# An attention and expert kernel whose order is planned: no filler matmuls before the first turning of keys, and 366 priorities set anew

## The chip, the core and the metric

The kernel runs on one core of one Trainium2 chip. A core has five engines that run side by side and wait for one another by semaphores: TensorE (PE in the profile, its weight loads apart as PEld), VectorE (DVE), ScalarE (ACT), GpSimd (POOL) and SyncE (SP), which issues most of the DMA transfers. Each engine takes its instructions strictly in the order in which the program holds them. The metric is the time of the launch in device microseconds, as the median of the runs.

## What is computed

Two stages, of which the second works on the result of the first. For each of four batches, 49 agents attend to 11456 keys and values, and then the queries attend to the agents; every token of the result goes to one of eight experts, the one with the largest logit, and through that expert's two layers.

```python
B, N, C = (4, 11456, 128)                      # 49 agents
def _attn_ref(q, k, v, agents):
    def sm(a, b):
        s = scale * (a @ b.transpose(0, 2, 1))
        e = np.exp(s - s.max(-1, keepdims=True))
        return e / (e.sum(-1, keepdims=True) + 1e-09)
    return sm(q, agents) @ (sm(agents, k) @ v)
...
logits = x @ w_gate                            # x: the result, 45824 x 128; 8 experts, hidden 1024
expert_idx = np.argmax(logits, axis=1)
for e in range(E):
    h = np.maximum(x[expert_idx == e] @ w1[e], 0.0)
    out[expert_idx == e] = gate_w[expert_idx == e, None] * (h @ w2[e])
```

## The kernel before

**Tiling.** A batch's 11456 tokens are cut into 12 chunks (11 of 1024 tokens as 128 partitions by 8, and a rest of 192). `key_chunk` adds the work of one chunk of keys: a load of k and one of v (512 KB each), two *turnings* of four 128x128 blocks each by TensorE (`turn`, line 593, in the first batch into a PSUM bank called px), their copies to SBUF by VectorE and ScalarE (`turned`, line 601), the scores of the agents against the keys (`kscores`, line 614), the running maximum (line 619), the exponentials (line 631), a turning back (`eback`, line 637) and the product with the values (`values`, line 652), which is added up in `acc`. Only three buffers (`vt`) hold values, so the load of chunk c+3 waits for `values` of chunk c. When all 12 are done, `agentvalues` (named av 0 to av 10) finishes the agents' values and multiplies them with the gate; `choose` finds the batch's commonest expert, whose weights are loaded. The steps named w (lines 905 to 1100) rewrite that expert's layers so that most tokens can pass through a small version of it. Queries are scored against the agents (lines 743 to 776), exponentiated (781), split in two halves (789, 794), turned by DMA into the tiles `M`, and routed (`logits`, line 838; `route`, lines 851 to 864).

**The expert stage.** `layer1` (L1, lines 1648 and 1649), `upper` and `lower` (lines 1655 and 1660), `linear` (L0) and `layer2` (L2, both line 1664), `store` (line 1709) and `put` run for 23 groups of 512 tokens per batch; `check` (ck, cx, lines 1677 and 1682) finds tokens for which the small version is not exact. Those, and the tokens of other experts, are gathered in 20 blocks of 128 rows (`prepare_blocks`, named g, lines 1437 to 1504) that go through the full layers (b1, bu, b2, lines 1525 to 1543). The stages of the four batches overlap: while batch b is in its expert stage, the attention of b+1 runs between.

**What sets the order.** Nothing is ordered by hand. Every step is added to a `Plan` with a rank, an engine, a planned cost, the steps it waits for and the buffers that it takes and frees. `Plan.order` walks through planned time: whenever an engine is free it takes the ready step of the lowest rank. The list that comes out is the program's order. Ranks come from a few numbers per part (`KS1, KT1`, `QA`, `RG`, `CK0`, `CK3`, `LTL`, `STAGES`) plus a table, `SHIFT`, that moves single steps. Planned costs and times decide the order alone; the chip takes its own time.

**Fillers.** Where TensorE would be idle in planned time for more than `FILL_GAP`, a spare matmul without use, `warm` (line 461 until the first linear, later line 465), is put into its row, so that the engine stays busy. They start in planned time zero, when the constant tile `place` that they read is the only thing they need.

Of the kernel before, what the change touches and what calls it, by code (L numbers as in the profile page):

```python
# [44 lines left out]
KS, KT, KS1, KT1 = -102.41, 5.86, -136.97, 9.15  # L45
KS0, KT0 = -300, 4
QA, QC, QC3, QA1, QA3 = -30.13, 6.23, 4.1, -23.65, -25.3
QD = (0, 0.5, 1, 1.5, 2, 5, 5.3, 5.8, 6.2, 6.6, 6.9)
LL, RG = 2.23, 1.22
# [5 lines left out]
CK0, CK1, CK2, CK3 = -0.61, 7.51, 2.21, 3.19  # L55

LT, LTS, LTL = 73.41, 2, 37.18
# [6 lines left out]
STAGES = ((2, 11, -69.39, -69.39 + 6, 4.97, -2.93, 5.65), (3, 6, 20.99, 20.99 + 2, 10, 63.79, 4.01), (4, 3, 30.77, 30.77 + 2, 0, 85.1, 3.87))  # L64
# [5 lines left out]
FILL, FILL_GAP = 0.25, 0.15  # L70
STICK = 1.91
# [14 lines left out]
    (1, 'w', 'c0'): 2.73, (1, 'qwhole', 3): 2.73, (1, 'ehigh', 2): 2.73, (2, 'kmax', 1): 2.73, ('L0', 1, 14): 1.69, (1, 'put', 13): 1.69,  # L86
    ('cx', 1, 8, 1): 1.69, (1, 'enorm', 11): 1.69, (2, 'eback', 11): 1.69, ('L2', 74): 1.69, (1, 'eturn', 10): 1.69, (2, 'ecopy', 11): 1.69,
# [4 lines left out]
    (0, 'estore', 0): -0.44, ('ranks', 2, 0, 3): -3.38, (1, 'kcorr', 9): -3.86, ('cx', 0, 10, 0): 13.27, (1, 'qexp', 0): 13.27,  # L92
    (1, 'ehigh', 0): 13.27, (2, 'route', 8, 3): 0.71, (2, 'qexp', 10): 0.71, ('L1', 121): 0.71, (2, 'ehigh', 10): 0.71, (2, 'factors', 8): 0.71,
# [6 lines left out]
    (0, 'w', 'lm'): -0.16, (0, 'route', 0, 3): -0.16, (0, 'factors', 0): -0.16, (1, 'kmax', 0): -0.16, (0, 'eback', 9): 0.84, ('cx', 1, 5, 1): 6.52,  # L100
# [3 lines left out]
    (3, 'estore', 3): -12.27, ('L1', 157): -1.69, ('L2', 27): -1.76, (0, 'enorm', 11): -1.76, (0, 'estore', 11): -1.76, (1, 'vsum', 10): -1.76,  # L104
# [13 lines left out]
}  # L118


class Plan:
# [24 lines left out]
    def order(self):  # L146
# [9 lines left out]
        turn = {p: [] for p in self.strict}  # L156
# [35 lines left out]
        while left:  # L192
# [4 lines left out]
            for g in engines:  # L197
# [15 lines left out]
                e = best  # L213
# [1713 lines left out]
```

## Time and profile before

| | us |
|---|---|
| median of 3 runs | 730.42 (728.89 to 731.21) |
| the profiled execution, whole | 726.68 |
| its span, first to last instruction | 725.0 |
| TensorE busy | 673.6 (93%) |
| VectorE busy | 551.1 (76%) |
| ScalarE busy | 499.8 (69%) |
| GpSimd busy | 272.2 (38%) |

The profiled execution was 3.74 us shorter than the median of the timed runs. In the rows further below a time is in microseconds from the start of the span; a row of the timeline has start, duration, engine, line, operation, tiles written and read, and in brackets how long the engine was idle before it and what ended that. Rows of stretches give each engine's busy time, then the clock that the throttle granted TensorE as a share of 2.4 GHz, the share of the 16 DMA engines, and GB/s.

### The profile page before, as it was taken

What the parts mean: (1) busy time and instruction counts of PE and PEld (TensorE: products, weight loads), DVE (VectorE), ACT (ScalarE), POOL (GpSimd) and SP (SyncE); (2) the same over time, 40 slices, a digit from 0 to 9 for tenths busy, and PEclk for the clock granted to TensorE, in tenths of its full rate; (3) what the DMA queues carried; (4) which work ended last, traced back from release to release, by engine and by line L of the source; (5) the groups of instructions that cost most, each with busy time, mean ns of one, the idle gap of its engine ahead of it and who ended that gap; (6) DMA issues with size and microseconds to landing.
All of it is one profiled execution on the core that took longest, in us unless ns stands there. A gap on an engine that the chain in (4) does not pass through costs nothing. (4 is left out here: it accounts for less than half of the span.)

```text
span 725.0 us, 20869 instructions
## 1 busy us (share of the span) xinstructions
PE 673.6 (93%) x7844; PEld 528.2 (73%) x7844; DVE 551.1 (76%) x1545; ACT 499.8 (69%) x1145; POOL 272.2 (38%) x454
## 2 busy tenths in 40 slices
PE   7999899999999999999999999989699999999993
PEld 3675477777776677777767776676588788989992
DVE  4558767778789777688897888788998699987630
ACT  2555579997775889887766989868554997633330
POOL 1002313222168403111586053355888245241331
PEclk9999999999999999999999999999989999999997
DMA  8946999997492899997846999978967999876850
GB/s 296 332 142 185 271 236 239 289 233 230 140 308 84 239 306 253 285 186 208 272 127 172 285 255 274 242 186 230 247 180 185 237 244 239 209 236 211 257 177 16
DMA packets 219928, 162.11 MB, mean 224 GB/s; under 512 B 110363, under 2 KB 193661, under 8 KB 219824
## 3 DMA queue, kind: packets, MB, share of 16 engines
q1 hardware_dynamic: 216400, 156.41, 81.1%
q0 software_dynamic: 2240, 3.29, 2.5%
q8 instruction: 63, 1.03, 0.6%
q10 hardware_dynamic: 1184, 1.05, 0.5%
q14 instruction: 41, 0.34, 0.2%
HBM read 98.51 MB, written 36.82 MB: 187 GB/s over the span
## 5 line engine op out<-in xcount | busy, mean ns | idle before, releaser
L1664 PE MATMUL py<-W,hh 128*128 128x128 f16 x2160 | 146.2, 220 | 0.1
L1660 DVE SCALAR_TENSOR_TENSOR hh<-ph,hh 128x512 f16<-128x512 f32 (+1 forms) x184 | 121.5, 670 | 29.8 <-ACT hh L1655 29.5
L1664 PEld LDWEIGHTS <-hh 128*128 128x128 f16 x2160 | 129.6, 99 | 12.1 <-issue 7.8
L1655 ACT ACTIVATE hh<-ph 128x512 f16<-128x512 f32 (+1 forms) x184 | 106.6, 591 | 34.0 <-PE ph L1649 33.9
L1682 ACT ACTIVATE jk<-ps_small 128x512 f16<-128x512 f32 x180 | 108.7, 604 | 15.6 <-PE ps_small L1677 13.9
L799 POOL TENSOR_TENSOR sq<-E 128x392 f32<-128x392 f32 (+1 forms) x48 | 41.9, 874 | 205.2 <-ACT E L781 205.2
L1709 DVE TENSOR_TENSOR yo<-py,cs 128x512 f32<-128x512 f32 (+1 forms) x92 | 61.8, 671 | 15.3 <-PE py L1664 14.9
L601 ACT COPY xT<-ps_small 128x512 f32<-128x512 f32 (+1 forms) x99 | 55.5, 591 | 19.1 <-PE ps_small L593 19.0
L1648 PE MATMUL ph<-M,Wah 128*128 128x512 f16 (+1 forms) x162 | 60.7, 375 | 2.7 <-DVE hh L1660 2.4
L1649 PE MATMUL ph<-M,Wal 128*128 128x512 f16 (+1 forms) x162 | 60.7, 374 | 0.0
L593 PE MATMUL ps_small<-ident,ld 128*128 128x128 f32 x390 | 56.9, 276 | 3.9 <-DMA ld<-in_k_dram 2.4
L1677 PE MATMUL ps_small<-Wck,M 128*128 128x256 f16 x318 | 54.4, 273 | 2.0 <-ACT jk L1682 1.5
L1664 PEld LDWEIGHTS <-M 128*128 128x128 f16 x636 | 40.1, 98 | 21.4 <-issue 16.9
L1664 PE MATMUL py<-Wl,M 128*128 128x128 f16 x636 | 49.3, 220 | 5.5 <-DVE yo L1709 5.3
L593 PEld LDWEIGHTS ps_small<-ident,ld 128*128 128x128 f32 x390 | 43.7, 142 | 12.3 <-issue 3.8
L794 POOL TENSOR_TENSOR mm<-E,mm 128x392 f16<-128x392 f32 (+1 forms) x48 | 43.2, 902 | 19.5 <-ACT mm L789 11.3
L652 PE MATMUL ps_small<-vt,SS 128*49 128x129 f32 (+1 forms) x720 | 49.5, 278 | 0.9 <-ACT SS L643 0.5
L614 PE MATMUL ps_small<-xT,agf 128*64 128x512 f32 (+3 forms) x192 | 48.2, 579 | 1.3 <-ACT xT L601 1.1
L652 PEld LDWEIGHTS ps_small<-vt,SS 128*49 128x49 f32 (+1 forms) x720 | 39.1, 130 | 11.8 <-issue 4.2
L1677 PEld LDWEIGHTS <-M 128*128 128x128 f16 x318 | 28.7, 98 | 23.2 <-issue 10.1
L631 ACT ACTIVATE ET<-ps_small,nm 113x512 f32<-113x512 f32 (+1 forms) x48 | 31.6, 661 | 18.2 <-DVE nm L621 16.2
L1531 ACT ACTIVATE hs<-ph 128x512 f32<-128x512 f32 x40 | 23.3, 597 | 28.7 <-PE ph L1525 28.7
(335 smaller groups left out, 1551.8 us busy)
## 6 DMA issues: line engine op xcount, KB each, us to landing
ld<-in_k_dram SPq DMA_DIRECT2D x44, 512.0 KB
vt<-in_v_dram SPq DMA_DIRECT2D x44, 512.0 KB
ld<-in_q_dram SPq DMA_DIRECT2D x44, 512.0 KB
out_dram<-yo SPq DMA_DIRECT2D x88, 256.0 KB
w1e<-in_moe_w_dram SPq DMA_DIRECT2D x23, 512.0 KB
w2e<-in_moe_w_dram SPq DMA_DIRECT2D x23, 512.0 KB
exps<-E SPq DMA_DIRECT2D x44, 196.0 KB
ranks<-C SPq DMA_DIRECT2D x4, 724.0 KB
```

The source lines that it names most:

```text
L593: nc.tensor.transpose(pt[:, i * p:(i + 1) * p], x[:p, h + i, :], ident[:p, :p])
L601: (nc.scalar.copy if eng == "A" else nc.vector.tensor_copy)(TT[src, c][:, h:h + n, :p], pv)
L614: nc.tensor.matmul(ps[64 * j:64 * j + w, :n * p], AG["f"][:, :w], x[:, j * n:(j + 1) * n, :p], start=True, stop=True)
L652: nc.tensor.matmul(ps[r:r + w, :D + 1], s[:p, i, r:r + w], x[:p, j * n + i, :], start=i == 0, stop=i == n - 1)
L1648: nc.tensor.matmul(ph[:, :nn], st['ah'][:, f, :], m, start=True, stop=False)
L1649: nc.tensor.matmul(ph[:, :nn], st['al'][:, f, :], m, start=False, stop=True)
L1655: nc.scalar.activation(hh[:, 0, :nn], ph[:, :nn], AF.Relu)
L1660: nc.vector.scalar_tensor_tensor(hh[:, 1, :nn], ph[:, :nn], 0.0, hh[:, 0, :nn], op0=ALU.max, op1=ALU.subtract)
L1664: mm_ = lambda o, l, r, **k: nc.tensor.matmul(o, l, r, skip_group_check=True, **k)
L1677: nc.tensor.matmul(ps[:p, i * (FD - FN):(i + 1) * (FD - FN)], st['M'][c][:, 2 * j + i, :p], st['ck'].rearrange("a f p -> a (f p)"), start= ...
L1682: nc.scalar.activation(jk[:p, :2 * (FD - FN)], hs.pop(("c", c, j))[:p, :2 * (FD - FN)], AF.Relu, scale=-1.0, accum_out=st["fl"][:p, 4 * c ...
L1709: nc.vector.tensor_tensor(yo[:p, :n, :], py[:p, :n * D].rearrange("p (i d) -> p i d", d=D), cs.unsqueeze(2).broadcast_to([p, n, D]), op=AL ...
```

## The change

Two lines of `Plan.order` and its numbers. (a) No filler goes in until `FILL_FROM`, the second turning of the first chunk of keys, has been placed (`self.begun`). (b) TensorE counts as busy in planned time until 2.4. (c) Nine numbers of parts change (`KS1`, `KT1`, `QA`, `RG`, `CK0`, `CK3`, `LTL` and the ranks in `STAGES`), and the table `SHIFT` is replaced by one with 366 entries, of which a line is shown.

```diff
-KS, KT, KS1, KT1 = -102.41, 5.86, -136.97, 9.15
+KS, KT, KS1, KT1 = -102.41, 5.86, -130.54, 8.69
-QA, QC, QC3, QA1, QA3 = -30.13, 6.23, 4.1, -23.65, -25.3
+QA, QC, QC3, QA1, QA3 = -28.84, 6.23, 4.1, -23.65, -25.3
...
+PE_FROM, FILL_FROM = 2.4, (0, "turn", "k", 0, 4)
...
+    ('L2', 35): -2.03, ('L1', 161): -0.53, ('L0', 3, 10): -0.53, ('L2', 158): -0.53, ('L2', 159): -0.53, ('L1', 162): -0.53, ('b1', 9, 0): -1.75,
...
+        self.begun = False
...
         busy = {g: 0.0 for g in engines}
+        busy["PE"] = PE_FROM
...
+                self.begun = self.begun or e["name"] == FILL_FROM
...
-            if busy["PE"] <= t + 1e-9 and min(nxt) - t > FILL_GAP:
+            if self.begun and busy["PE"] <= t + 1e-9 and min(nxt) - t > FILL_GAP:
```

The work is the same but for the spare matmuls: 104 before, 87 now (66 and 53 of line 461 and its successor, line 492; 38 and 34 of the later kind). All lines behind the table stand 31 lines further down. What moves is shown at three places, before and then now.

TensorE, the start of the program: `sa` holds the agents' squares, `ag` the agents, `ld` a chunk of keys. Ten spares stand ahead of the first of these rows and three more behind the last.

```order
L461 LDWEIGHTS place
L461 MATMUL warm<-place 128x512
L514 MATMUL ps_small<-sa,ones 128x1
L515 MATMUL ps_small<-ident,ag 128x49
L461 LDWEIGHTS place
L461 MATMUL warm<-place 128x512
```

```order
L545 MATMUL ps_small<-sa,ones 128x1
L546 MATMUL ps_small<-ident,ag 128x49
L624 MATMUL px<-ident,ld 128x128 x8
L492 LDWEIGHTS place
L492 MATMUL warm<-place 128x512
```

Fourteen spares ahead of the first eight turnings are gone; the four behind them stay, and so do the next four.

ScalarE, batch 3, where its agents' values are finished while batch 2 is in its expert stage: `gj` squares the gate product, `E` and `mm` are the query exponentials and their upper half.

```order
L1655 ACTIVATE hh<-ph 128x512
L601 COPY xT<-ps_small 128x512
L789 CAST mm_160<-E 128x8x49
L781 ACTIVATE E<-E,ln_70,div 128x392
L789 CAST mm_161<-E 128x8x49
L702 ACTIVATE gj,gss<-ps_small 128x8
```

```order
L1713 ACTIVATE jk,fl<-ps_small 96x512
L1686 ACTIVATE hh<-ph 128x512
L733 ACTIVATE gj,gss<-ps_small 128x8
L735 COPY ava<-ps_small 49x128
L1686 ACTIVATE hh<-ph 128x512 x2
L812 ACTIVATE E<-E,ln_70,div 128x392
```

`gj` stood behind an exponential and its halves and now stands ahead of them.

VectorE, the same place a little later: `fm`, `fgt` belong to a block being prepared, `mq` and `E` to a chunk of queries, and L412 (now L443) is the first of the instructions that make `Gs`, the split gate that `logits` multiplies.

```order
L1477 TENSOR_TENSOR fm<-fm,fg 128x270
L1478 TENSOR_REDUCE fgt<-fm 128x3
L551 TENSOR_SCALAR hb<-ss 128x1
L771 TENSOR_REDUCE mq<-ps_small 128x4
L772 TENSOR_TENSOR E<-ps_small,mq 128x196
L771 TENSOR_REDUCE mq<-ps_small 128x4
L772 TENSOR_TENSOR E<-ps_small,mq 128x196
L412 TENSOR_SCALAR hb<-ps_small 128x1
```

```order
L1508 TENSOR_TENSOR fm<-fm,fg 128x270
L1509 TENSOR_REDUCE fgt<-fm 128x3
L443 TENSOR_SCALAR hb<-ps_small 128x1
L446 TENSOR_SCALAR mul<-hb 128x1
L449 TENSOR_SCALAR div<-hb 128x1
```

Five instructions on queries no longer stand between the block and the gate.

## Rows read from the trace of the kernel before

**Rows 1.** Busy time by stretch: columns as told above, PE to POOL
```profile
19.00:50.00 31.00, 31.00 (x300) 22.16 (x300) 17.82 (x43) 18.17 (x43) 0.00 (x0) 1.00 0.84 265
57.40:91.90 34.50, 30.32 (x261) 18.16 (x261) 26.96 (x94) 20.89 (x39) 11.42 (x22) 1.00 0.88 247
91.90:706.00 614.10, 584.44 (x7093) 469.01 (x7092) 492.55 (x1355) 450.83 (x1045) 255.27 (x408) 0.99 0.88 227
```

**Rows 2.** Waits of TensorE between 91.9 and 706: in total, times, longest
```profile
PE py L1664 <- DVE yo L1709: 5.5, 10, 1.9
PE ps_small L838 <- DVE Gs L716: 3.5, 1, 3.5
```

**Rows 3.** Timeline of TensorE, first 13 us
```profile
4.89 4.18 PE L461 MATMUL warm<-place 128*128 128x512 f16 x10 [4.89 <-DVE place L365]
...
9.31 1.04 PE L461 MATMUL warm<-place 128*128 128x512 f16 x4
...
10.18 1.04 PE L593 MATMUL px<-ident,ld 128*128 128x128 f32 x8
...
11.06 1.03 PE L461 MATMUL warm<-place 128*128 128x512 f16 x4
...
12.01 1.07 PE L614 MATMUL ps_small<-xT,agf 128*64 128x512 f32 x4
```

**Rows 4.** Timeline of VectorE and ScalarE there: the agents and the copies of turned keys
```profile
2.89 0.22 DVE L501 TENSOR_SCALAR ag<-ag 49x128 f32<-49x128 f32 x1 [0.57 <-DMA ag<-in_agents_dram]
...
3.37 0.19 ACT L510 ACTIVATION_READ_ACCUMULATOR jk<-ag 49x1 f32 x1
...
11.26 0.59 ACT L601 COPY xT<-px 128x512 f32<-128x512 f32 x1 [6.73 <-PE px L593]
```

**Rows 5.** Busy time by stretches at the start; here the last two columns count, the DMA's
```profile
0.00:4.00 4.00, 0.00 (x0) 0.00 (x0) 2.35 (x17) 1.69 (x3) 2.14 (x19) 1.00 0.36 76
4.00:8.00 4.00, 3.11 (x8) 1.26 (x9) 0.93 (x8) 0.32 (x1) 0.00 (x0) 1.00 0.99 323
8.00:12.00 4.00, 4.00 (x23) 2.27 (x20) 1.67 (x6) 0.59 (x1) 0.39 (x2) 1.00 1.08 340
12.00:28.00 16.00, 15.91 (x137) 10.98 (x137) 8.40 (x17) 8.64 (x19) 0.00 (x0) 1.00 1.07 374
```

**Rows 6.** Timeline of TensorE: values of chunk 3, of chunk 10, the first expert matmul
```profile
32.62 1.10 PE L652 MATMUL ps_small<-vt,SS 128*64 128x129 f32 x16
...
51.00 1.31 PE L652 MATMUL ps_small<-vt,SS 128*64 128x129 f32 x20 [0.35 <-DMA vt<-in_v_dram]
...
91.88 0.39 PE L1648 MATMUL ph<-M,Wah 128*128 128x512 f16 x1
```

**Rows 7.** Busy time of TensorE by the turnings of line 593 alone
```profile
19.00:50.00 31.00, 9.98 (x74) 7.85 (x73) 1.00 0.84 265
```

**Rows 8.** Timeline of TensorE where batch 3's agents' values are finished
```profile
517.65 0.38 PE L707 MATMUL ps_small<-gss,ones 128*128 128x1 f32 x2 [2.05 <-ACT gj L702]
...
524.77 0.36 PE L838 MATMUL ps_small<-Gs,M 128*128 128x18 f16 x8 [3.55 <-DVE Gs L716]
```

**Rows 9.** Timeline of VectorE there, from the agents' sum to the gate
```profile
511.31 0.22 DVE L693 TENSOR_REDUCE avs<-av 128x1 f32<-128x64 f32 x1
511.44 1.28 DVE L571 SCALAR_TENSOR_TENSOR hl<-ld,mul,hl 128x1024 f16<-128x1024 f32 x1
...
522.31 0.14 DVE L551 TENSOR_SCALAR hb<-ss 128x1 int32<-128x1 int32 x1
...
523.70 0.15 DVE L412 TENSOR_SCALAR hb<-ps_small 128x1 int32<-128x1 int32 x1
...
524.59 0.68 DVE L1660 SCALAR_TENSOR_TENSOR hh<-ph,hh 128x512 f16<-128x512 f32 x1
```

**Rows 10.** Stretches around two low grants of the clock
```profile
472.90:476.30 3.40, 3.37 (x36) 3.33 (x36) 2.41 (x7) 2.05 (x6) 2.81 (x6) 0.50 0.57 161
524.10:530.90 6.80, 5.93 (x35) 5.88 (x36) 6.40 (x20) 1.93 (x5) 6.38 (x10) 0.50 0.82 246
```

More of the change, by code (lines that the diff above doesn't have):

```diff
@@ L43 @@
 WHOLE = ((0, 1, 2), (0, 1, 2, 3, 4), (0, 1, 2, 3, 4), (0, 2, 4, 6, 8))
-KS, KT, KS1, KT1 = -102.41, 5.86, -136.97, 9.15
+KS, KT, KS1, KT1 = -102.41, 5.86, -130.54, 8.69
 KS0, KT0 = -300, 4
-QA, QC, QC3, QA1, QA3 = -30.13, 6.23, 4.1, -23.65, -25.3
+QA, QC, QC3, QA1, QA3 = -28.84, 6.23, 4.1, -23.65, -25.3
 QD = (0, 0.5, 1, 1.5, 2, 5, 5.3, 5.8, 6.2, 6.6, 6.9)
-LL, RG = 2.23, 1.22
+LL, RG = 2.23, 1.26
 TE = -14.49
@@ L54 @@
 LAG = 3
-CK0, CK1, CK2, CK3 = -0.61, 7.51, 2.21, 3.19
-LT, LTS, LTL = 73.41, 2, 37.18
+CK0, CK1, CK2, CK3 = -0.59, 7.51, 2.21, 3.38
+LT, LTS, LTL = 73.41, 2, 34.5
 RC = 9
@@ L63 @@
 PACE = (2, 4)
-STAGES = ((2, 11, -69.39, -69.39 + 6, 4.97, -2.93, 5.65), (3, 6, 20.99, 20.99 + 2, 10, 63.79, 4.01), (4, 3, 30.77, 30.77 + 2, 0, 85.1, 3.87))
+STAGES = ((2, 11, -70.36, -70.36 + 6, 4.76, -2.66, 5.75), (3, 6, 23.98, 23.98 + 2, 10, 63.79, 2.77), (4, 3, 27.31, 27.31 + 2, 0, 85.48, 4.91))
 HIGH = (0, 1, 2, 3)
 FILL, FILL_GAP = 0.25, 0.15
+PE_FROM, FILL_FROM = 2.4, (0, "turn", "k", 0, 4)
 STICK = 1.91
@@ L80 @@
 SHIFT = {
[5 rows of a table removed]
-    (1, 'w', 'c0'): 2.73, (1, 'qwhole', 3): 2.73, (1, 'ehigh', 2): 2.73, (2, 'kmax', 1): 2.73, ('L0', 1, 14): 1.69, (1, 'put', 13): 1.69,
-    ('cx', 1, 8, 1): 1.69, (1, 'enorm', 11): 1.69, (2, 'eback', 11): 1.69, ('L2', 74): 1.69, (1, 'eturn', 10): 1.69, (2, 'ecopy', 11): 1.69,
[4 rows of a table removed]
-    (0, 'estore', 0): -0.44, ('ranks', 2, 0, 3): -3.38, (1, 'kcorr', 9): -3.86, ('cx', 0, 10, 0): 13.27, (1, 'qexp', 0): 13.27,
-    (1, 'ehigh', 0): 13.27, (2, 'route', 8, 3): 0.71, (2, 'qexp', 10): 0.71, ('L1', 121): 0.71, (2, 'ehigh', 10): 0.71, (2, 'factors', 8): 0.71,
[6 rows of a table removed]
@@ L100 @@
-    (0, 'w', 'lm'): -0.16, (0, 'route', 0, 3): -0.16, (0, 'factors', 0): -0.16, (1, 'kmax', 0): -0.16, (0, 'eback', 9): 0.84, ('cx', 1, 5, 1): 6.52,
[3 rows of a table removed]
-    (3, 'estore', 3): -12.27, ('L1', 157): -1.69, ('L2', 27): -1.76, (0, 'enorm', 11): -1.76, (0, 'estore', 11): -1.76, (1, 'vsum', 10): -1.76,
[13 rows of a table removed]
[3 rows of a table added]
+    ('ranks', 0, 0, 2): 2.73, (2, 'turned', 'k', 1): 2.73, (1, 'qmax', 2): 2.73, (0, 'put', 20): 2.73, ('up', 45): 2.73, (2, 'eback', 0): 2.73,
+    ('lo', 45): 2.73, (1, 'qexp', 2): 2.73, (1, 'w', 'm'): 2.73, ('L0', 0, 21): 2.73, (1, 'w', 'sq'): 2.73, ('ranks', 0, 0, 3): 2.73,
@@ new lines @@
+    ('L2', 42): 2.73, (1, 'estore', 2): 2.73, (1, 'w', 'cp'): 2.73, (1, 'w', 'u'): 2.73, ('L2', 43): 2.73, (1, 'w', 's2'): 2.73,
+    (2, 'kscores', 1): 2.73, ('ranks', 0, 0, 4): 2.73, (2, 'ecopy', 0): 2.73, (1, 'w', 'c0'): 2.73, (1, 'qwhole', 3): 2.73, (1, 'ehigh', 2): 2.73,
[3 rows of a table added]
+    ('ranks', 3, 0, 12): -0.77, ('lo', 164): -0.77, ('ranks', 3, 0, 13): 1.97, (3, 'store', 11): 1.97, (3, 'qscores', 11): 9.66, ('L2', 151): 9.66,
[4 rows of a table added]
+    (0, 'kscores', 4): -0.78, (0, 'kmax', 3): -0.78, (0, 'values', 2): -0.78, (0, 'kmax', 4): -0.78, (0, 'kexp', 3): -0.56, (0, 'kcorr', 3): -1.34,
[3 rows of a table added]
@@ new lines @@
+    ('ck', 1, 6, 3): 3.79, (2, 'kcorr', 8): 3.79, (2, 'eback', 8): 3.79, (1, 'squares', 10): 3.79, (1, 'store', 9): 3.79, ('L1', 72): 3.79,
+    (1, 'put', 9): 3.79, ('L0', 1, 10): 3.79, (2, 'ecopy', 8): 3.79, (1, 'hb', 10): 3.79, (1, 'scaling', 10): 3.79, ('L2', 66): -0.21,
+    ('cx', 1, 6, 1): 3.79, (1, 'upper', 10): 3.79, (2, 'values', 8): 3.79, ('up', 70): 3.79, (2, 'turn', 'k', 9, 0): 3.79, (1, 'lower', 10): 3.79,
[5 rows of a table added]
+    ('ranks', 2, 0, 6): -0.39, (3, 'turn', 'q', 6, 0): -0.39, (3, 'ehigh', 3): -0.39, (3, 'estore', 4): -0.39, (3, 'turn', 'q', 6, 4): -0.39,
[3 rows of a table added]
@@ new lines @@
+    (2, 'estore', 5): 0.1, (3, 'load', 'k', 7): 0.1, (2, 'turn', 'q', 7): 0.1, (2, 'eturn', 0): 5.96, (1, 'put', 18): 5.96, (2, 'load', 'q', 3): 5.96,
[21 rows of a table added]
+    (0, 'turn', 'k', 2, 4): 2.55, (0, 'eback', 1): 2.55, (0, 'turn', 'k', 3, 0): 2.55, (0, 'kscores', 2): 2.55, (0, 'values', 1): 2.55,
+    (0, 'turn', 'k', 3, 4): 2.55, (0, 'turn', 'k', 4, 0): 2.55, (0, 'turn', 'k', 4, 4): 2.55, (0, 'eback', 2): 2.55, (3, 'turned', 'k', 4): 1.76,
+    ('L0', 2, 2): 1.76, ('up', 99): 1.76, ('L2', 96): 1.76, ('cx', 2, 2, 0): 1.76, ('lo', 99): 9.71, (3, 'values', 3): 1.76, (2, 'squares', 6): 1.76,
@@ new lines @@
+    ('L2', 24): 0.56, ('L1', 59): -0.19, (1, 'qscores', 6): -0.19, (2, 'values', 5): -0.19, (2, 'kscores', 6): -0.19, ('L2', 57): -0.19,
+    ('ck', 1, 3, 2): -0.19, ('L1', 60): -0.19, (3, 'qmax', 4): -1.68, (2, 'turn', 'k', 2, 0): -0.75, (0, 'qexp', 10): -0.37, (2, 'eback', 7): -0.48,
+    (2, 'kscores', 5): -1.68, (1, 'turn', 'q', 7): -1.68, ('ck', 1, 3, 0): -1.68, (0, 'turned0', 'k', 10): -0.24, ('b1', 19, 1): -13.15,
+    ('b2', 19): -13.15, ('up', 162): 0.27, (2, 'logits', 8): -0.7, ('L1', 120): -0.7, (3, 'kscores', 11): -0.7, ('L0', 2, 12): -0.7,
@@ L118 @@
+    (3, 'eback', 10): -0.7, ('L2', 116): -0.7, (0, 'vsum', 2): 0.22, (0, 'load', 'v', 5): 0.22, (0, 'kexp', 4): 0.22, (0, 'eback', 3): 0.22,
+    (0, 'turned0', 'k', 5): 0.22, (1, 'turned', 'k', 11): -8.96, ('bu', 13, 0): -1.37, ('cx', 2, 2, 1): 0.11, (3, 'kexp', 4): 0.11,
+    (3, 'kcorr', 4): 0.11, ('up', 101): 0.11, (3, 'ecopy', 4): 0.11, (2, 'squares', 7): 0.11, (0, 'put', 2): -5.81, ('up', 4): -3.35,
+    ('up', 5): -3.35, (0, 'qexp', 4): -3.35,
 }
```

72 rows, old and new, of the table SHIFT are left out of this document.

## The prediction

> **What bounds the kernel now.** I read the busy times of each engine first, then by stretch, then what TensorE waits for, and then the timeline wherever a wait or an idle stretch is moved by the change. TensorE is busy 93% of the span, and the stretches show how evenly: in the first batch's keys it has no idle time at all (31.00 of 31.00), and in the expert stages 584.44 of 614.10, so that 29.66 us of waits are all there is to win between 91.9 and 706 [rows 1]. Those waits are scattered; ten of them, for the buffer that `store` frees, make 5.5, the longest 1.9, and a single one, for the split gate `Gs`, makes 3.5 [rows 2]. VectorE, at 76%, decides TensorE's time only where something stands in its row ahead of what TensorE needs. So the time is TensorE's row of work plus its waits plus what it loses at the low clock, and a start that comes x earlier is worth x, if nothing behind eats it.
>
> The start is the other loss. TensorE's first useful matmuls stand behind ten spares: these run from 4.89 to 9.07, and the first eight turnings of keys run only from 10.18, with four more spares ahead of them; their four behind, then the first scores at 12.01 [rows 3]. The spares show the clock: the ten take 0.42 us each, the later four 0.26 each with the end of the last, so the clock stands at the lower level (1.2 GHz) through nearly all of the ten and at the upper (2.4 GHz) from about 9 on. (The clock column reads 1.00 throughout there; I go by the spacing.)
>
> **(a) and (b): no spares ahead of the first turnings.** When could these start? They need the first chunk of keys. The agents come first in TensorE's row, and their inputs are there early: VectorE had the agents at 2.89, ScalarE their squares by 3.56 [rows 4]. The chunk's landing isn't in the rows by itself, but the bytes are: 0.30 MB moved by 4.0, 1.29 more by 8.0 [rows 5]. The first key chunk is the first of the 512 KB loads (0.52 MB); with the small constants ahead of it, it is moved at about 4 + 0.25/0.323 = 4.8 if served in order, and later if the loads share the engines. What lies between the last bytes and the reader no row shows; the agents' whole load had its reader at 2.89 [rows 4], so it can't be long. I add 0.8, a choice, and take 5.6 for the first turning, with 4.8 and 6.4 as ends.
>
> What follows runs at the low level, since nothing has run before. The eight turnings took 0.88 from their start to the next work at the upper level [rows 3], so 1.8; the four spares behind them, at the 0.42 of the ten, 1.7. The copies of the turned keys, which the scores need, take 0.59 after the turnings [rows 4] and lie beside the spares. So the scores start at 5.6 + 1.8 + 1.7 = 9.1, against 12.01 [rows 3]: 2.9 earlier. Against that stands the clock. Before, it rose while the last of the ten spares ran, at about 9, and TensorE had begun at 4.89; it now begins up to 0.7 later, so I take the rise at 9.6, half a microsecond into the scores, and half of that, 0.25, is lost. Then the next turning: it takes the second key chunk, the third of the loads, 1.6 MB in all, moved by 8.0 [rows 5]; it is needed only at about 10. Some 0.15 goes for a short gap. The term is **-2.5**, with ends -3.3 (start at 4.8) and -0.8 (start at 6.4, and two microseconds more at the low level).
>
> Does the lead live? The loads run at a share of 1.07 until 28 [rows 5]. The values of chunk 3 are the sixteenth load: 1.6 + 1.36 + 16 x 0.374 = 8.9 MB are moved by 28, so its 8.5 MB by about 27, while TensorE came to them at 32.62 [rows 6]. 2.5 earlier is 30.1: still 3 behind the transfer. Later loads of values wait for a buffer that `values` of three chunks earlier frees, so they move with TensorE; the last waited 0.35 on its load already, at 51.00 [rows 6], with the DMA at 0.84 on average [rows 1]. There the lead can be lost in part; I take none. Between 57.4 and 91.9 TensorE waits for 4.2 us [rows 1], on chains that begin with the agents' values and so move along. Then the first expert matmul comes at 89.4, not 91.88 [rows 6].
>
> **(c) the new numbers.** Nearly all of the 366 shifts swap neighbours. One place is worth a term: batch 3's agents' values. `gj` goes ahead of an exponential on ScalarE, and the 2.05 that TensorE waited for it [rows 8] can go. But the gate needs VectorE's row as well, and that is what ends last: 12.4 us of unbroken work from the sum of agents' values at 511.31 to the gate's first instruction at 523.70 [rows 9]. What goes from between them, by the order: the lower half of a chunk of queries, 1.28, and one norm and four steps on queries, from 522.31 to 523.70, 1.39. What comes in: a `store` and a `lower`, 0.6 each at the spacing of such a one at 524.59 (0.68 with its end) [rows 9]. Net -1.4. TensorE's work between the same two points, 7.8 before, is 7.7 by the same list: so its waits there go from 6.3 in all to about 5.0. **-1.3**; the 2.05 comes back as a longer wait for `Gs`. The ends are 0 (VectorE is held by something else first) and -6.3 (the wait goes altogether, which would take VectorE's chain to be no longer than TensorE's work).
>
> For the rest I take **0**. Between equal swaps the size is that of one pair: the longest wait on `store` is 1.9 [rows 2], and the low clock that came with it ran 3.40 us at 0.50 [rows 10], so half, 1.7, is lost. One such pair less or one more is -3.6 or +3.6. At the end of the program a block's second layer (18) slips between the two layers of block 19, with the same matmuls behind the last group's: nothing.
>
> **Sum.** -2.5 - 1.3 + 0 = -3.8 on the profiled 726.68, or 722.9. The median lies 3.74 above the profiled execution; taking the change to be the same there, 730.4 - 3.8 = **726.6**.
>
> **Rivals.** *The clock comes up late, and the kernel is slower.* The spares ran without a break; now turnings, four spares, scores and waits for copies stand there, with gaps. Each microsecond at the low level loses half of one. If the level stays low until T, the loss beyond the term is (T - 9.6)/2. The whole gain of 3.8 is gone at T = 17.2, and the kernel is slower by 2.2 at T = 21.6. At T = 24, say, it gives +3.4, or 733.8. For it: the low stretches around 473 and 524 followed waits of about 2 and 3.5 us on TensorE and held for 3.4 and 6.8 [rows 10]. Against it: from 12 on TensorE is busy 15.91 of 16 [rows 5], and that work stays as it is.
>
> The Trainium skill has a rule for it: "TensorE: Matmul & The Clock Gate", Part 4 (PE-mode transpose), says that transposes don't count as work for the clock in the way other matmuls do, so that they don't bring it to its full rate. By that rule the first eight turnings would add nothing and the clock would wait for scores and values. As a mechanism of this kernel: the rise then goes with the scores, which begin at 9.1, and not with the turnings ahead of them; before, it went with spares that began at 4.89 and came at about 9. As far behind the scores it comes at about 13, and the loss is (13 - 9.6)/2 = 1.7: -2.1 in all, or 728.3, a shade within what counts as no difference below. The trace bears on it: between 19 and 50, 9.98 of 31 us were turnings, and the clock stayed at the upper level [rows 1, 7]; so a third of turnings among other work doesn't lower it, but a start from turnings is not shown. I count it in the next case.
>
> *The lead is absorbed.* By the loads (the wait of 0.35 at 51.00 becomes 2.9) or in part by a clock that comes up near 13. Then only the 1.3 remains: 729.1, within 0.3%, which is about 2.2 us and what a measurement of this kernel can tell from no change. For it: the DMA is at its limit until 28 and near it behind. Against it: the buffers free earlier.
>
> *More than that goes.* If the wait for `store` near 473 and its low clock go (-3.6), and half of the low stretch near 524 with the shorter wait (6.8 us at 0.50 lose up to 3.0, for 5.93 of it was busy; half is 1.5) [rows 10], the sum is -8.9, or 721.5.
>
> *The neighbours fall badly.* One more pair of wait and low clock, +3.6, leaves 730.2: no difference; two, 733.8.
>
> That the change doesn't do what it says can be left out: the order shows the turnings without their spares, and the gate without its five instructions.
>
> **How the numbers follow.** Forecast (-2.2 to -6, 724.4 to 728.2): 0.48. Better: 0.14. Absorbed, a late clock of the smaller kind, or one bad pair: 0.24. Slower, by the late clock (0.08) or by the neighbours (0.06): 0.14. So faster by over 0.3% has 0.62, within 0.24, slower 0.14. For 8 in 10 the range takes the forecast's, nearly all of the middle case, and half of each side: 720.5, the better case with the start at its early end, to 732.0, which is the late clock at T = 20.4. The forecast's own range is 724.4 to 728.2.
>
> **What would show it.** In the profile after: first turning at 4.8 to 6.4 (later: the load was the bound); scores at 9 to 10; spares 0.42 apart at 7.5, and 0.22 by 11; values of chunk 3 near 30 with no wait; of chunk 10 near 48.5 with a wait under 0.5; the first expert matmul near 89.4. The waits of TensorE from the agents' sum to `logits` of batch 3 near 5.0, nearly all for `Gs`. The clock's records near 470 and 524 tell which of the cases on neighbours holds. Wrong are: turnings at a low clock beyond 12 (the rival), a long wait on a load of values before 51, or waits between 92 and 706 whose sum moves by more than 4 us from 29.7 without either place above.

## The result and the profile after

The changed kernel took 720.45 us (median of 4 runs, 719.53 to 720.99) against 729.65 for the kernel before beside it: a ratio of 0.9877, 95% interval 0.9843 to 0.9910, or 9 us less where 3.8 were forecast. Timed again later it was 0.9895 (0.9867 to 0.9922). The profiled execution has a span of 717.8 and took 719.53 in all, so it lies 0.9 below its median, not 3.7 as before; the two profiled executions are 7.2 apart.

The start, in the timeline of TensorE (start, duration, engine, line, operation, tiles, idle time and what ended it), up to the first expert matmul; it answers to [rows 3] and [rows 6]:

```profile
4.38 0.59 PE L545 MATMUL ps_small<-sa,ones 128*128 128x1 f32 x2 [4.38 <-ACT jk L541]
...
5.57 1.97 PE L624 MATMUL px<-ident,ld 128*128 128x128 f32 x8 [0.34 <-DMA ld<-in_k_dram]
7.34 1.91 PE L492 MATMUL warm<-place 128*128 128x512 f16 x4
9.18 1.24 PE L645 MATMUL ps_small<-xT,agf 128*64 128x512 f32 x4
10.35 1.09 PE L624 MATMUL px<-ident,ld 128*128 128x128 f32 x8
...
30.03 1.10 PE L683 MATMUL ps_small<-vt,SS 128*64 128x129 f32 x16
...
48.14 1.32 PE L683 MATMUL ps_small<-vt,SS 128*64 128x129 f32 x20 [0.86 <-DVE xT L632]
...
90.09 0.39 PE L1679 MATMUL ph<-M,Wah 128*128 128x512 f16 x1
```

The first turning starts at 5.57, bound by its load; turnings and spares run at the lower clock level; the scores start at 9.18, where 12.01 stood; chunk 3's values come 2.6 earlier without a wait. The values of chunk 10 come 2.86 earlier. One microsecond is lost again between there and the first expert matmul, which comes 1.8 earlier.

The expert stages, as busy time by stretch (length, then PE, PEld, DVE, ACT, POOL, the granted clock, DMA share, GB/s), against [rows 1] and [rows 10]; and VectorE's busy time on the page:

```profile
90.00:700.00 610.00, 585.39 (x7104) 470.05 (x7101) 483.42 (x1357) 451.87 (x1044) 254.04 (x408) 0.99 0.89 228
20.00:511.30 491.30, 469.39 (x5638) 352.28 (x5637) 387.36 (x1043) 383.66 (x884) 179.30 (x310) 1.00 0.89 232
511.35:524.95 13.60, 12.29 (x94) 10.31 (x94) 10.28 (x34) 5.31 (x12) 11.92 (x16) 0.50 0.83 258
```

```profile
PE 669.9 (93%) x7827; PEld 527.1 (73%) x7827; DVE 541.2 (75%) x1545; ACT 501.4 (70%) x1145; POOL 271.0 (38%) x454
```

Three things are to be seen. TensorE's idle time in the stages is 24.6 us now, 29.7 before. The low grant near 473 is gone (1.00 from 20 to 511.3), and the other has grown from 6.8 to 13.6 us. And VectorE is busy 541.2 us for its 1545 instructions, where the same 1545 took 551.1: the stages' row fell from 492.55 to 483.42. That I had not looked for.

The place of batch 3's agents' values: TensorE's waits from 90 to 700 first (in total, times, longest), then VectorE's timeline, then the stretch from the agents' sum to the product with the gate, against [rows 2], [rows 8] and [rows 9]:

```profile
PE py L1695 <- DVE yo L1740: 4.5, 10, 0.7
...
PE ps_small L869 <- DVE Gs L747: 0.4, 1, 0.4
```

```profile
502.76 0.22 DVE L724 TENSOR_REDUCE avs<-av 128x1 f32<-128x64 f32 x1
...
504.37 0.31 DVE L1321 SCALAR_TENSOR_TENSOR far<-z,cb,q 128x90 f32<-128x90 f32 x1
...
512.07 0.15 DVE L443 TENSOR_SCALAR hb<-ps_small 128x1 int32<-128x1 int32 x1
```

```profile
502.76:513.11 10.35, 6.50 (x98) 5.43 (x98) 9.15 (x40) 4.83 (x13) 6.08 (x13) 0.91 1.03 234
```

From the sum to the gate VectorE needs 9.31 us, 12.39 before and 11.0 by the forecast. The order gives 1.4 of the 3.1; the rest is instructions that are there in both and are shorter now, the 0.31 above most of all. In the kernel before it took 1.44, while GpSimd ran a 128x720 operation from 513.07 to 515.82; in the changed kernel that operation was over (499.23 and 2.74) when the 0.31 began. The row of VectorE, then of GpSimd, then the stretch, all of the kernel before:

```profile
513.25 1.44 DVE L1290 SCALAR_TENSOR_TENSOR far<-z,cb,q 128x90 f32<-128x90 f32 x1
```

```profile
513.07 2.75 POOL L1299 TENSOR_SCALAR C<-d 128x720 f32<-128x720 f32 x1
```

```profile
511.31:524.77 13.46, 7.18 (x102) 5.49 (x100) 12.59 (x44) 7.39 (x17) 11.62 (x20) 0.98 0.89 259
```

### The profile page after: what moved, and what is told of

It reads as the page before. It is cut to its first block, busy times and chain, and to the rows that moved or that the text cites. A ratio compares the mean times of both kernels' runs of the same rounds, so it can differ in the third digit from the quotient of the medians.

```text
span 717.8 us, 20820 instructions
## 1 busy us (share of the span) xinstructions
PE 669.9 (93%) x7827; PEld 527.1 (73%) x7827; DVE 541.2 (75%) x1545; ACT 501.4 (70%) x1145; POOL 271.0 (38%) x454
## 5 line engine op out<-in xcount | busy, mean ns | idle before, releaser
L830 POOL TENSOR_TENSOR sq<-E 128x392 f32<-128x392 f32 (+1 forms) x48 | 39.8, 828 | 197.6 <-ACT E L812 197.5
L602 DVE SCALAR_TENSOR_TENSOR hl<-ld,mul,hl 128x1024 f16<-128x1024 f32 (+1 forms) x30 | 37.3, 1242 | 17.4 <-ACT hl L597 17.2
L1556 PE MATMUL ph<-fxT,w1e 128*128 128x128 f32 x320 | 43.1, 280 | 1.7 <-DVE hh L1691 1.0
```

The lines of the kernel that those rows point to most:

```text
L1556: nc.tensor.matmul(ph[:, i * P:(i + 1) * P], w[:, hf * 4 + i, :], blocks[u][0], start=True, stop=True)
```

## The experiments

To follow a gain through a program, I took in each trace the start of the same instructions and subtracted the time of the profiled kernel before: TensorE's product with the gate (lines 697 and 728) for batches 0 and 1, VectorE's 54th store, and TensorE's last matmul; minus is earlier. These are single executions.

```
                                 gate 0   gate 1   54th store   TensorE's end   VectorE busy
kernel before (us)                 56.1    204.1        443.5           712.9          551.1
changed kernel                     -2.8     -3.5         -4.0            -7.8          541.2
changed kernel, timed again        -2.4     -3.1         -3.6            -3.7          541.6
start alone                        -1.7     -1.8         -1.9            +2.1          551.8
numbers alone                      +0.2     -1.7         -2.3            -6.3          541.1
after, then before                 -2.9     -3.6         -4.7            -2.5          551.2
squares back                       -3.3     -4.1         -4.8           -10.3          540.8
gate spares                        -1.9     -3.1         -3.8            -7.6          542.2
early spares                       -3.4     -4.1         -4.7            -9.7          542.9
```

In the changed kernel's two executions the first three columns repeat to within a microsecond; behind the 54th store the two differ by four. So sizes are taken from the timed ratios, and the table says only where.

**The start alone.**

```diff
-        for e in plan.order():
-            e["f"](*e["a"])
+        steps = plan.order()
+        first = next(i for i, e in enumerate(steps) if e["name"] == (0, "turn", "k", 0, 0))
+        for i, e in enumerate(steps):
+            if i < first and e["name"][0] == "fill":
+                continue
+            e["f"](*e["a"])
```

> The kernel before, its order kept row for row, with the 14 spares ahead of the first turnings taken out: part (a) alone. Theory (the start term of the prediction, now with the traces): the first turning at 5.6, the first scores at 9.2, TensorE 2.8 ahead at the gate of batch 0 (53.4 for 56.15), 1.8 to 2.8 ahead at the end, so -1.8 to -2.8 us against the kernel before, ratio 0.996 to 0.9975; the low grants near 470 and 522 stay as they were (3.4 and 6.8 us). Rival 1 (the start carries most of the 9 us, because what follows falls differently behind it): -6 or more, with the low grant near 470 gone. Rival 2 (the lead is eaten): 0 to -1.

726.92 us, 0.9966 (0.9940 to 0.9993): 2.5 us less. Its timeline of TensorE:

```profile
5.51 1.97 PE L593 MATMUL px<-ident,ld 128*128 128x128 f32 x8 [1.06 <-DMA ld<-in_k_dram]
...
9.11 1.97 PE L614 MATMUL ps_small<-xT,agf 128*64 128x512 f32 x4
11.01 1.34 PE L593 MATMUL px<-ident,ld 128*128 128x128 f32 x8
```

The lead of the theory holds at the start, and the ratio gives its size, but loosely: the interval runs from 0.5 to 4.4 us, and the medians are 1.2 apart (728.12 for the kernel before). The two low grants stay as they were (3.4 and 6.8 us). The first scores ran wholly at the lower level here (1.97), in the changed kernel only in part (1.24): the clock came up some 2 us later in this execution, which goes with a lead of 1.7 at the gate and not 2.8. Nothing of the 1.7 is lost up to the first expert matmul (90.07, 1.8 earlier than before).

**The numbers alone**, ten spares and four put back in the changed kernel:

```diff
+            for _ in range({(0, "agsum"): 10, (0, "turn", "k", 0, 0): 4}.get(e["name"], 0)):
+                keep_warm()
             e["f"](*e["a"])
```

> The changed kernel, its order kept row for row, with ten spares put back ahead of the agents and four ahead of the first turnings: parts (b) and (c) alone. Theory (the new numbers carry the larger part): the first scores at 12.0 again and the rest as in the changed kernel, 1.8 to 2.8 us slower than it, so -6.4 to -7.4 us against the kernel before, ratio 0.990 to 0.991. Rival (the start carries it): -1.3 to -3 against before, ratio 0.996 to 0.998, and a low grant of the clock near 470 again.

723.77 us, 0.9945 (0.9915 to 0.9975): 4.0 us less, fewer than expected and three times the 1.3 of the prediction. VectorE's 541 us come with the numbers, not with the start. 2.5 and 4.0 are 6.5 of the 7.6 to 9 of the whole, within the intervals.

**The numbers of the first part, those of the second part of the kernel before.** `ORDER` is a written list of the steps: the changed kernel's up to the store of group 6 of batch 2, and what is left in the order of the kernel before, with its spares from there on:

```diff
-        for e in plan.order():
-            e["f"](*e["a"])
+        by = {e["name"]: e for e in plan.order()}
+        for n in ORDER:
+            if n == "F":
+                keep_warm()
+            elif n == "L":
+                keep_warm_later()
+            else:
+                by[n]["f"](*by[n]["a"])
```

> The changed kernel's order up to the store of group 6 of batch 2 (at about 423 of 718 us), and from there on the order of the kernel before. Theory (by the lead that the two traces show: 4.2 to 4.6 us at 420, of them 2.8 from the start; another 2.7 at the pair near 470; nothing at batch 3's agents' values): 4 to 4.6 us below the kernel before, ratio 0.9937 to 0.9945, with the low grants near 470 and 520 of the kernel before. Rival (most of the gain lies behind 423): no more than the start, 2 to 3 us, ratio 0.996 to 0.997. Other rival (all of it lies ahead): 8 us or more.

723.73 us, 0.9949 (0.9924 to 0.9974), so 3.7 us of the 7.6 that the changed kernel gained beside it lie ahead of the cut: 2.5 the start, some 1.2 the numbers. The other 4, by the difference, lie behind it, and VectorE is at 551.2 again: its 10 us go with the order behind the store of group 6. The wait near 470 is back, but not the low grant; and at batch 3's agents' values, where the old order stands again, the grant is as long as in the changed kernel (timeline of TensorE, then the two stretches):

```profile
467.72 0.61 PE L2045 MATMUL py<-Wl,M 128*128 128x128 f16 x8 [1.90 <-DVE yo L2090]
```

```profile
466.00:471.00 5.00, 3.28 (x65) 3.07 (x65) 4.90 (x11) 2.75 (x6) 4.42 (x9) 1.00 0.94 224
513.85:527.45 13.60, 10.59 (x82) 10.30 (x83) 12.71 (x41) 4.29 (x9) 12.13 (x17) 0.50 0.91 268
```

A wait of 1.9 us is followed by a low grant in one execution and not in another, and a low grant of 13.6 us doesn't need the new order.

**That wait taken away in the kernel before**, by one swap on VectorE:

```diff
-        for e in plan.order():
+        steps = plan.order()
+        for name, anchor, behind in [((2, "store", 11), (3, "kmax", 10), 0)]:
+            e = next(x for x in steps if x["name"] == name)
+            steps.remove(e)
+            i = next(i for i, x in enumerate(steps) if x["name"] == anchor)
+            steps.insert(i + behind, e)
+        for e in steps:
             e["f"](*e["a"])
```

> The kernel before with one step moved: VectorE stores group 11 of batch 2 ahead of the running maximum of batch 3's chunk 10, whose one-column instruction took 1.72 us there while GpSimd ran two products of its own. Theory (that pair of wait and low grant near 473 costs 1.88 and about 1.7 us): the wait for that store shrinks to under 0.5, the low grant of 3.4 us near 473 is gone, and the time is 2 to 3.5 us below the kernel before, ratio 0.995 to 0.997. Rival (what is behind has slack, or the exponentials of the keys become late instead): the grant is gone and the time within 1 us of the kernel before.

727.88 us, 1.0005 (0.9980 to 1.0031). The rival holds. The grant near 473 is gone, and TensorE waits for the exponentials that it turns back instead (timeline of VectorE, of TensorE, and two stretches):

```profile
469.85 0.68 DVE L1709 TENSOR_TENSOR yo<-py,cs 128x512 f32<-128x512 f32 x1
...
471.16 1.14 DVE L621 TENSOR_TENSOR nm<-nm 113x1 f32<-113x1 f32 x1
```

```profile
473.08 0.61 PE L637 MATMUL ps_small<-ident,ET 113*128 113x113 f32 x4 [1.47 <-ACT ET L631]
```

```profile
472.90:476.30 3.40, 3.22 (x63) 3.01 (x64) 3.19 (x9) 2.29 (x7) 2.83 (x6) 1.00 0.90 235
518.20:531.80 13.60, 10.68 (x81) 10.40 (x82) 12.83 (x43) 4.97 (x10) 11.57 (x15) 0.50 0.83 254
```

So the 3.6 us at which the prediction priced that pair are not there to be had by itself: in the timed runs this swap bought nothing. Why is open in part: the wait came back as another, and the low grant at batch 3's agents' values is 13.6 us long in this execution, 6.8 in the kernel before, so the clock won near 473 may have been lost there.

**The squares put back** behind the exponential and its half, in the changed kernel, with the same loop; beside it, the changed kernel itself, with no edit:

```diff
+        for name, anchor, behind in [((3, "av", 7), (3, "ehigh", 1), 1), ((3, "av", 8), (3, "av", 7), 1), ((3, "av", 10), (3, "av", 7), 1)]:
```

> The changed kernel itself, beside the next three on the same chip. Theory: 0.986 to 0.990 of the kernel before, as it measured; the low grants in the profile again one near 511 of 10 us or more and none near 470. Rival (the low grants fall as chance has it): one near 470 again, or none near 511.

> The changed kernel with one step of batch 3's agents' values put back: ScalarE squares the gate product behind the exponential of chunk 1 and its upper half again, and TensorE's sum of the squares goes one place further back with it. Theory (VectorE's row decides when the split gate is ready, so the early squares only moved the wait): the wait for the squares of about 2 us is there again, the gate's first instruction on VectorE comes within 0.5 us of where it came, 9.3 us behind the agents' sum, and the time is within 1 us of the changed kernel's. Rival (the 2.05 us that TensorE waited for the squares were a true cost): 1.5 to 2.5 us slower than the changed kernel.

721.25 us, 0.9895 (0.9867 to 0.9922), for the changed kernel, with a low grant of 13.6 us from 515.15 on and none near 470, as expected; 721.05, 0.9913 (0.9887 to 0.9939), with the squares back. TensorE waits, and the gate comes 9.08 us behind the sum all the same (timelines of TensorE and VectorE, squares back):

```profile
510.51 0.38 PE L738 MATMUL ps_small<-gss,ones 128*128 128x1 f32 x2 [1.57 <-ACT gj L733]
```

```profile
503.82 0.22 DVE L724 TENSOR_REDUCE avs<-av 128x1 f32<-128x64 f32 x1
...
512.90 0.15 DVE L443 TENSOR_SCALAR hb<-ps_small 128x1 int32<-128x1 int32 x1
```

As the prediction said: the wait for the squares only stands in front of the wait for the gate. By the traces that swap is worth nothing by itself; the timed runs show no difference (1.3 us by the ratios, 0.2 by the medians, the intervals overlap).

**Spares in the waits of that place**, 30 of 256 columns, into unused columns of the gate's tile:

```diff
+        def spare_gate(n):
+            for _ in range(n):
+                nc.tensor.matmul(GATE[3][:, 2 * P:], place[:, :P], place[:, :2 * P], start=True, stop=True)
+
+        extra = {(3, "qscores", 1): 10, (3, "turn", "q", 4, 4): 14, (3, "qscores", 3): 6}
         for e in plan.order():
+            for _ in range(extra.get(e["name"], 0)):
+                spare_gate(1)
             e["f"](*e["a"])
```

> The changed kernel with 30 spares of 256 columns in TensorE's row at the place where batch 3's agents' values are finished (10 ahead of one chunk's query scores, 14 ahead of a turning of queries, 6 ahead of the next scores), written into unused columns of the gate's own PSUM tile; they fill the waits of 1.10, 1.49 and 0.67 us there. Theory (the waits bring the clock down from 511.4 to 524.1, 12.7 us with 11.4 busy, so about 5.7 us lost): with the waits filled the clock stays at the upper level there at least until 520, and the time is 3 to 5.7 us below the changed kernel's. Rival (the clock falls for another reason, or VectorE's row decides the end of that place anyway): still a low grant of 10 us or more, less than 1 us gained.

719.10 us, 0.9880 (0.9852 to 0.9908), no other than the changed kernel's 0.9877 and 0.9895 (which were not timed beside it), though the low grant is gone. The stretch, and TensorE behind it:

```profile
500.00:530.00 30.00, 24.82 (x304) 21.09 (x303) 25.34 (x82) 17.69 (x41) 23.28 (x35) 1.00 0.97 253
```

```profile
521.72 0.61 PE L1697 MATMUL py<-Wl,M 128*128 128x128 f16 x8 [1.80 <-DVE yo L1742]
...
529.74 0.35 PE L993 MATMUL ps_small<-wcmp,ones 128*128 128x32 bf16 x8 [1.23 <-DVE wcmp L981]
```

With the waits filled the clock stays up. But TensorE then waits longer for VectorE: 0.88 for the gate (0.40 in the changed kernel), 1.80 for the store (0.71), 1.23 for `wcmp` (none). Half of the 12.29 us that TensorE was busy under the low grant is some 6 us; 2.8 of them are back as such waits within 20 us, and where the remainder went the runs don't show. The theory's step from waits to a low grant came in this execution; the 3 to 5.7 us that it expected did not.

**Early spares**, which read a constant that is there at 1.2:

```diff
+    def keep_warm_early():
...
+        nc.tensor.matmul(warm[0], ones16, ones16.unsqueeze(1).broadcast_to([P, 4, P]), start=True, stop=True)
...
         for e in plan.order():
+            for _ in range({(0, "agsum"): 7, (0, "turn", "k", 0, 0): 1}.get(e["name"], 0)):
+                keep_warm_early()
             e["f"](*e["a"])
```

> The changed kernel with seven spares ahead of the agents' matmuls and one ahead of the first turning, which read a constant that is there at 1.2 us and so end before the first chunk of keys lands. Theory (the first turnings and scores run at the lower clock level for want of work ahead of them, not for being turnings): spares 0.43 apart from 1.3 on, the upper level by about 5.5, the eight turnings in 0.9 to 1.1 instead of 1.77, the four spares behind in 0.9 instead of 1.7, the first scores at 7.4 instead of 9.18; then the second turnings wait for their load until 8.5 to 9.2, so 1.1 to 1.9 us ahead of the changed kernel at the gate of batch 0 and as much less time at the end. Rival (the loads bound the start, or the lead is eaten behind): the second turnings no earlier than 10, less than 0.5 gained.

717.95 us, 0.9886 (0.9855 to 0.9917). In the timeline of TensorE the clock is up with the turnings, as expected, and the scores start at 7.70:

```profile
1.27 3.17 PE L497 MATMUL warm<-ones 128*128 128x512 bf16 x7 [1.27 <-DVE ones L351]
...
5.81 1.09 PE L629 MATMUL px<-ident,ld 128*128 128x128 f32 x8 [0.34 <-DMA ld<-in_k_dram]
...
7.70 1.07 PE L650 MATMUL ps_small<-xT,agf 128*64 128x512 f32 x4
...
47.58 1.32 PE L688 MATMUL ps_small<-vt,SS 128*64 128x129 f32 x20 [1.14 <-DMA vt<-in_v_dram]
```

Of the 1.5 us at the scores 0.6 are left at the gate of batch 0, since the values of chunk 10 wait 1.14 for their load; the second turnings come at 9.22, so the rival is wrong about the start and right about the end: no difference that the runs show.

**Four more**, beside which the kernel before took 743.53 us where it had taken 727.5 to 729.7: each is compared with that alone.

> The changed kernel with eight early spares once more, beside the next on the same chip, so that the two differ by the gate's spares alone. Theory: the first scores at 7.7 again, the gate of batch 0 at 52.7 to 53.3, since the last values of batch 0 wait about 1.1 us for their load; a low grant near 511 of 6 us or more; 0.985 to 0.989 of the kernel before.

> The same with the 30 spares at batch 3's agents' values as well. Theory (what is lost at the low clock there is mostly lost in the shadow of VectorE's row and of the loads, since 30 spares took the low grant away and the time stayed within 1 us): no low grant between 500 and 530, a longer wait for the store behind it, and the time within 1.5 us of the kernel without these spares. Rival (the low grant of 12.7 us with 11.4 busy costs its 5.7 us, and the earlier comparison was blurred by two chips): 3 us or more below the kernel without them.

> The order of the kernel before up to the store of group 6 of batch 2, and from there on the order of the changed kernel, start included in the first part. Theory (the parts add up: the changed kernel's 7.6 to 9 us less the 3.7 that its order up to that store gave): 3.5 to 5 us below the kernel before, ratio 0.993 to 0.995, without a low grant near 470. Rival (the later part only passes on the lead, and the change lies in the start and the early numbers): 0 to 2 us, ratio above 0.997.

> The changed kernel without the six spares that it still has between the first turnings and the first turning back: up to there TensorE has eight turnings, four matmuls of scores and eight turnings, with waits for the copies between. Theory (the clock rises on any matmuls of TensorE, turnings too, about as soon as with the spares): the first scores at 8.2 instead of 9.18, the upper level by 11, and the gate of batch 0 no later than in the changed kernel; time within 1 us of it. Rival (turnings don't count for the clock, or the waits for copies keep it low): turnings of 1.7 us or more and scores of 1.9 still behind 12, the gate of batch 0 1 to 3 us later than in the changed kernel.

The early spares gave 742.89, 0.9996 (0.9969 to 1.0023); with the gate's spares 740.46, 0.9961 (0.9935 to 0.9987); the kernel before up to the store and the changed one from there (the two lists of the splice swapped) 750.31, 1.0061 (1.0035 to 1.0087); the changed kernel without the six spares between the first turnings and the first turning back (left out as in the first experiment, up to `(0, "eback", 0)`) 743.97, 0.9999 (0.9975 to 1.0023). None of the expected ratios came. Three of these four hold all the new numbers and the start without the fourteen spares; two of them take as long as the kernel before, and the third 2.9 us less: the gain of 9 us isn't there in this series. The kernel before has no profile in it, nor was the changed kernel timed there by itself. Against the earlier profile of the kernel before, the early spares' lead at the 54th store is 3.8 (4.7 in their first execution), and from there to the end it is lost. This execution has pauses that the earlier one doesn't have. In the first of them GpSimd issues indirect transfers, as it does at the same place in the earlier one; VectorE (first row) and ScalarE start nothing for 3.63 and 2.92 us, and TensorE (second fence) stops for 0.36 to 0.39 between four matmuls and the next four:

```profile
466.20 0.57 DVE L811 TENSOR_REDUCE mq<-ps_small 128x8 f32<-128x392 f32 x1 [3.63 <-remote]
```

```profile
464.61 0.39 PE L1700 MATMUL py<-W,hh 128*128 128x128 f16 x4 [0.39 <-issue]
465.35 0.38 PE L1700 MATMUL py<-W,hh 128*128 128x128 f16 x4 [0.36 <-issue]
```

The same instruction of VectorE waited 0.20 in the earlier execution of this kernel. What stops the engines there isn't shown: "issue" is time in which the profile sees nothing waited for. The other three kernels of the series have a like pause of VectorE there (3.55 to 3.74). That VectorE has its 543.1 us in the spliced kernel too, which is yet slower, says that the lower busy time doesn't always bring the gain. The low clock of the place isn't settled there either: the kernels with and without the gate's spares differ by 2.4 us, with intervals that overlap, and the one without had a low grant of only 3.4 us there (from 518.83 on).

One thing the last kernel shows by itself, in TensorE's timeline:

```profile
7.50 2.25 PE L645 MATMUL ps_small<-xT,agf 128*64 128x512 f32 x4
9.69 1.09 PE L624 MATMUL px<-ident,ld 128*128 128x128 f32 x8
```

With nothing but three small matmuls and eight turnings ahead of the scores the clock is up at 9.69, behind four matmuls of scores and as soon as with spares, and the gate of batch 0 comes at 51.7, 1.7 ahead of the changed kernel's.

## Why the prediction was right, and where it was short

The time, 720.45, came at the low edge of the predicted range (720.5, where the terms given for that end add up to 720.7), and outside the forecast's own 724.4 to 728.2.

**Right by its steps: the start.** 5.6 for the turning (5.57), 1.8 and 1.7 for turnings and spares (1.77 and 1.84 by their starts), 9.1 for the scores (9.18), the rise near 9.6, 30.1 for chunk 3 (30.03): the term of -2.5 measured -2.5 alone (0.9966, interval 0.5 to 4.4 us), a closer match than the interval bears out. Its least sure choice, the 0.8 for the landing, happened to fit: that was luck. The step "There the lead can be lost in part; I take none" held at the loads, 2.86 at the values of chunk 10 and 2.8 at the gate; the next one, that the waits up to the first expert matmul move along, was a little short, 1.8 there (89.4 forecast, 90.09 seen).

**Right in mechanism, wrong in size: the place of the gate.** That VectorE's row ends it, and the squares only move a wait, the squares put back show. TensorE's idle time from the sum to `logits` fell from 6.28 to 3.85, where 5.0 was forecast. VectorE's row got 3.1 shorter, not 1.4, since its instructions also got shorter; and TensorE's work there, which the prediction took at 7.8 before and 7.7 now, was 7.18 and 6.50. But TensorE stayed at the lower level for 13.6 us with 12.29 busy, and the prediction had no term for a longer low grant there. The two kernels with the old order at this place that show the same 13.6 say that it isn't the new order's doing alone.

**The step that failed is "for the rest I take 0".** It took the new table (378 entries by the kernel's text, not 366) as swaps of neighbours whose sizes cancel, and priced them by one pair of wait and low clock. The numbers measured -4.0 (interval 1.8 to 6.2) instead of -1.3. About 1.2 of it lies ahead of the store of group 6, the rest behind, where VectorE's same instructions take 10 us less in every kernel with the new order (541 to 543) than in every one with the old (551 to 552). The row of the kernel before was in view, 492.55 us of VectorE against 584.44 of TensorE, but no instruction's length was compared with that of its like: a one-column minimum of 1.72 us, the `far` of 1.44. The traces say where the 10 us lie. I took from each VectorE instruction the length that the shortest tenth of its like (same operation, tile and shape, in all the traces) stays within, and summed what is over: for those with a GpSimd instruction beside them it is 36.1 us before and 26.5 now, for the others 3.7 and 3.3 (GpSimd's times in the profile are rough). As many have one beside them, 718 and 715, so the new order doesn't meet GpSimd less often, but loses less where it does. How much of the 10 us reaches the end isn't measured by itself; that the 4 us come from it is argued from where both appear, and in the last four runs they didn't come.

**The rivals.** "More than that goes", 721.5, is the time that came, yet not by its reason: the pair near 473 did go, but taking it out of the kernel before gave nothing (1.0005), and the other low grant grew. The late clock didn't come: the scores end at the upper level, ahead of 10.35, where the rise was put at about 13 at the earliest. The rule of the Trainium skill against this change, from "TensorE: Matmul & The Clock Gate", Part 4 (PE-mode transpose), that transposes don't count for the clock like other matmuls, is neither shown nor refuted: no run has a rise behind turnings alone. In the changed kernel four spares and a part of the scores stand between the first turnings and the rise, and without the spares four matmuls of scores (7.50 to 9.69).

## What to carry to other kernels

Ask of filler work that is to raise TensorE's clock whether it stands ahead of real work that is ready: here the clock was up by 9.69 with turnings and scores alone, and what the turnings lost at the lower level was half of their own length. Before paying to keep the clock up in a stage, look whether another engine's row ends there; here at least 2.8 of some 6 us came back as waits for VectorE. When a table of priorities is replaced, compare how long the same instruction takes at different places on the engine next in line, and what runs beside it, for an order can change durations and not only waits. And time the kernels that are to be compared beside each other: the gain of 9 us wasn't there in a series in which the kernel before took some 15 us longer.

## What the runs showed of the hardware

- The clock's rise isn't tied to one delay. With the same early spares from 1.27 on, it was up at the first turnings in one execution (5.81, eight in 1.09) and not before the scores in another:

```profile
5.53 1.97 PE L629 MATMUL px<-ident,ld 128*128 128x128 f32 x8
...
9.14 1.60 PE L650 MATMUL ps_small<-xT,agf 128*64 128x512 f32 x4
```

- A low grant at one place varies from execution to execution and doesn't by itself set the time: gate spares 0 us, squares back 3.4, changed kernel 13.6 in the profiled executions, with medians of 719.10, 721.05 and 720.45. That the clock is free there isn't shown. In the 38 timed runs of the changed kernel, numbers alone, gate spares, squares back and early spares (their first series), each kernel taken by itself, a mean granted clock lower by 0.001 goes with 0.47 us more (standard error 0.08), where 0.001 of the 718 us is 0.72. The mean is of the whole span, and a pause can lower the clock as well as lengthen the run, so it doesn't say what causes what.
- VectorE's one-column minimum at line 621 took 1.72 us beside two operations of 128x392 on GpSimd from 470.54 to 472.25, and 1.14 when it started 0.6 later; it ended 0.03 behind GpSimd's second in both. The changed kernel's like took 0.51, most of that line 0.16. That the two engines hinder each other there is read from these rows and from the sum above alone; no run tried it. In the kernel before:

```profile
470.56 1.72 DVE L621 TENSOR_TENSOR nm<-nm 113x1 f32<-113x1 f32 x1
```

```profile
470.54 0.92 POOL L794 TENSOR_TENSOR mm<-E,mm 128x392 f16<-128x392 f32 x1
471.40 0.85 POOL L799 TENSOR_TENSOR sq<-E 128x392 f32<-128x392 f32 x1
```
